# Causal attention with decay and a gated convolution: loads of the first head pair first, the activation table loaded ahead, and every order, engine, bank and buffer planned anew

## The chip, the cores and the metric

The kernel runs on one core of one Trainium2 chip. The metric is device microseconds of one execution (us), median of the runs shown. Engines: PE is the matrix engine, ACT the scalar engine, DVE the vector engine, POOL the GpSimd engine, and SP the engine that issues most of the transfers. Each engine works through its own instructions strictly in program order.

## The reference

Inputs are q, k, v of shape (8, 8, 576, 64), s of shape (8, 8, 576) and three weight arrays. Scores with a decay go through a causal softmax; the result goes through a causal five-tap convolution gate and two projections.

```python
scores = scale * np.matmul(q, k.transpose(0, 1, 3, 2))
cum = np.cumsum(np.maximum(s, 0.0), axis=-1)
bias = -(cum[:, :, :, None] - cum[:, :, None, :])
scores = np.where(causal, -1e9, scores + np.minimum(bias, 0.0))
attn = softmax(scores)                       # rows sum to 1
x = (attn @ v).transpose(0, 2, 1, 3).reshape(B, S, H * D)
gate_pre = sum(conv_w[t] * x_shifted[t] for t in range(5))
out = (sigmoid(gate_pre) * (x @ w_val)) @ w_out
```

## The kernel before

The work is cut into 32 units n = 4b + p: batch b (8 of them) and head pair p (4 each). For one unit, Q and K of two heads are loaded as float32 into a staging buffer qkf (five of them; a buffer holds two pairs; one transfer of the first pairs is 288 KB), cast to bf16 into qkb (three buffers), transposed on PE (step qq), copied out of PSUM into QKT (qe), and multiplied (scores, steps s0, s1, s2, and s4 for the last 64 queries). ACT takes exp of 128 x 1024 scores at a time (e0, e1, e2, e4) into P, of which there are three buffers. The triangle on the diagonal is cleared in one of two ways: PE adds a pair of wide matmuls of the tile fut to the scores, or POOL clears P afterwards with an affine select (mk). The decay is put into V instead of the scores: a running sum of s on DVE (relu, scan, centre), a transpose (decT) and one exp (expw) give w, and POOL multiplies V by w into Vp (vp). Then av multiplies P by Vp on PE, DVE divides by the row sum (rec, nm), PE transposes (xt), one copy goes to xT (xe), and the convolution follows as taps t1 to t4 (DVE, or POOL with a product p2 to p4 before it), tanh on ACT (th), the value projection on PE (val), the gate product on DVE (glu), and per two batches nine blocks of the output projection (out), their copies (oe) and stores (st). The last four units are split in two halves (steps u and f, with a third index on the later steps).

What sets the order is one text, ORDER: a list of steps name:engine:slots written by a planner beforehand. S, G, T, A and V are SP, POOL, PE, ACT and DVE; slots are PSUM banks or buffer numbers. The loop at the end of main_path (L731 to L746) calls each step's function in that order, with the engine that the list names, so the list fixes each engine's instruction order, which engine does a cast or a copy, which bank and which buffer it uses. Nothing is reordered later. Steps wu are matmuls of the identity that nobody reads; they keep PE busy.

The names and lines that the prediction uses: load_qk (L425) issues Q or K transfers, and ld_first those of batch 0, one head pair and one of Q and K at a time; ld_qk loads Q and K of one or two pairs of a later batch; ld_v (L448, L449 for batch 0, L452 later) loads V; ld_s (L374) the decay input, ld_cw (L396) the convolution weights. Casts, copies and evacuations all go through the helper copy (L371). vprime is L455, scores are L476 and L489 (the latter the fut matmuls), exps(step) is L527, mask L550, av L565, rec L578, norm L584, tap_product L614 (ACT) and L616 (POOL), tap L627, L632 (DVE) and L635 (POOL), tanh L652, val L664, glu L673, outp L684, stores L692.

At the end the kernel tests whether its way of computing was safe for the data: check0 and check1 (L695 to L707) test the row sums, and check0 also squares the 20 weight ratios cwr and compares them (L700, L701); count (L710) counts on PE, count_out (L719) takes the minimum, and flag (L715) reads it, so that a branch can run a general version in a rare case. That version does not run here.

Of the kernel before, what the change touches and what calls it, by code (L numbers as in the profile page):

```python
# [213 lines left out]
glu.0.0:V val.2.1:T:3 ld_v.2.4:S t1.5:V:1 e0.9:A xt.6:T:5 ld_v.2.3:S glu.3.0:V p3.5:G:1 s1.9:T:0+1 glu.2.1:V xe.6:A
ld.3.0:S:3 s1.8:T:6+7 e1.9:A t1.6:V:3 qq.2.2:T:2+3 out.0.3:T:4 t3.5:G qe.2.2:A t4.6:V out.0.2:T:0 th.4:A:4 t3.6:V
p4.5:G:0 oe.0.3:A:0 ld_v.3.3:S s0.8:T:1+2:2 oe.0.2:A:1 t2.6:V ld.3.1:S:4 qq.2.3:T:3+4 p2.5:G:1 e0.8:A xt.7:T:0 qe.2.3:V
out.0.0:T:5 e1.8:A xe.7:V t2.5:G s2.8:T:1+2 t1.7:V:2 out.0.1:T:3 e2.8:A t3.7:V vp.2.0:G val.4.1:T:4 th.6:A:1 oe.0.1:V:2
s4.2.3:T:1+2 s2.9:T:6+7 oe.0.0:A:4 t2.7:V t4.5:G val.6.1:T:3 e4.2.3:A st.0.0:S val.7.1:T:5 glu.6.1:V e2.9:A ld_v.3.2:S
val.4.0:T:1 t4.7:V vp.2.2:G st.0.3:S av0.8:T:2+3 glu.4.1:V ld_v.3.0:S th.7:A:0 val.6.0:T:0 glu.4.0:V av.8:T vp.2.1:G
th.5:A:2 glu.6.0:V s0.11:T:6+7:0 glu.7.1:V s0.10:T:0+1:2 rec.8:V e0.11:A val.5.1:T:4 nm.8:V c.3.0:G:0 val.7.0:T:5  # L220
e0.10:A xt.8:T:2 glu.7.0:V s2.10:T:6+7 c.3.1:G glu.5.1:V val.5.0:T:3 e2.10:A xe.8:V s1.10:T:0+1 glu.5.0:V ld_v.3.4:S
mk.10:G s1.11:T:4+5 t1.8:V:0 out.0.7:T:3 e1.11:A ld_v.3.1:S vp.2.3:G t4.8:V av0.9:T:6+7 e1.10:A ld.5.0:S:0 av.9:T t3.8:V
qq.3.0:T:4+5 mk.11:G oe.0.7:A:5 av0.10:T:0+1 rec.9:V qe.3.0:A nm.9:V st.0.7:S av.10:T c.3.2:G:1 ld.4.1:S:1 s0.12:T:3+4:1
# [576 lines left out]
```

## Time and profile before

| | before |
|---|---|
| median of 3 runs | 184.66 us (184.64 to 185.24) |
| the profiled execution | 185.04 us |
| its span, first to last instruction | 183.0 us |
| granted TensorE clock, mean | 0.978 |
| HBM read, written | 30.57 MB, 9.44 MB |

The profiled execution's time is 2.04 us more than its span: what lies before its first and behind its last instruction. It is 0.38 us above the median of the three runs. A page of the profile has busy times by engine, forty slices of the span with the busy share of each engine, the chain of work that ended last, and groups of instructions. In the views a row "x3" stands for three instructions merged; the bracket at a row's end says how long the engine had been idle and what released it.

### The profile page before, as it was taken

Reading aid. Unit: us, or ns where it says so; the run is one execution under the profiler, and the core shown is the slowest. Engines: PE = TensorE matmul, PEld = TensorE weight load, DVE = VectorE, ACT = ScalarE, POOL = GpSimd, SP = SyncE. Lnnn points to the kernel's source line nnn. Section 1 sums busy time; section 2 is a strip of 40 time slices with the busy share of each in tenths; the row PEclk is TensorE's granted clock in tenths of the full one; section 3 lists DMA queues with packets and bytes.
Section 4 is the critical chain, followed back from the end, with each engine's and each line's share of the span. In section 5 each row is a group of like instructions: output and inputs, shape, how many; then the busy total and the mean of one; then the engine's idle time right before and its main releaser. Section 6 shows DMA issues by size and latency. Waiting matters only on the chain.

```text
span 183.0 us, 6744 instructions
## 1 busy us (share of the span) xinstructions
PE 166.4 (91%) x2773; PEld 108.8 (59%) x2790; DVE 161.3 (88%) x311; ACT 159.0 (87%) x229; POOL 158.9 (87%) x150
## 2 busy tenths in 40 slices
PE   6499889899999999999989999999899999999950
PEld 2136765667557765665856675775567746757520
DVE  4295699999999999999999999989999999999940
ACT  0098999898999899999999999899999899998830
POOL 5289689999999989999699999889999998999800
PEclk9879999999999999999999999999999999999995
DMA  5999999999999999975899958994960014006461
GB/s 140 332 288 317 296 189 283 399 362 185 295 345 253 298 334 318 333 205 127 244 306 271 326 153 273 224 249 116 222 216 4 4 57 176 3 4 236 170 238 56
DMA packets 52812, 40.48 MB, mean 221 GB/s; under 512 B 38885, under 2 KB 38885, under 8 KB 52778
## 3 DMA queue, kind: packets, MB, share of 16 engines
q1 hardware_dynamic: 52490, 39.42, 75.4%
q10 hardware_dynamic: 288, 0.59, 1.2%
q8 instruction: 23, 0.38, 0.9%
q14 instruction: 11, 0.09, 0.2%
HBM read 30.57 MB, written 9.44 MB: 219 GB/s over the span
## 4 chain that ended last, share of the span: by engine, by line
PE 73%; ACT 11%; DVE 4%; issue 3%; DMA 3%; SPq 2%; POOL 1%; ACTq 0%; DVEq 0%; POOLq 0%
PE bank L664 18%; PE bank L684 16%; PE bank L565 13%; PE bank L476 13%; ACT P L527 7%; PE bank L597 5%; PE bank L460 5%; DMA qkf<-in_q_dram 3%; PE bank L489 2%; POOL qkb L371 1%; DVE xn L584 1%; ACT QKT L371 1%; DVE gp L632 1%; ACT th L652 1%; SPq L425 1%
## 5 line engine op out<-in xcount | busy, mean ns | idle before, releaser
L527 ACT ACTIVATE P<-bank 128x1024 bf16<-128x1024 f32 x84 | 82.9, 1037 | 1.9 <-PE bank L476 1.6
L632 DVE SCALAR_TENSOR_TENSOR gp<-bank,cwr,gp 128x572 f32<-128x572 bf16 (+6 forms) x74 | 55.0, 753 | 1.0
L635 POOL TENSOR_TENSOR gp<-gp,pr 128x573 f32<-128x573 f32 (+6 forms) x34 | 41.1, 1212 | 4.3 <-DVE recs L578 2.3
L455 POOL TENSOR_TENSOR Vp<-vst,w 128x650 bf16<-128x650 f32 x32 | 40.7, 1287 | 1.2 <-DMA vst<-in_v_dram 1.0
L476 PE MATMUL bank<-QKT 64*128 64x128 bf16 (+5 forms) x592 | 39.1, 241 | 1.7 <-ACT P L527 1.3
L664 PE MATMUL bank<-xT,wv 128*128 128x288 bf16 (+2 forms) x256 | 38.9, 287 | 0.4 <-ACT P L527 0.2
L371 POOL CAST qkb<-qkf 128x1152 bf16<-128x1152 f32 (+2 forms) x29 | 31.8, 1120 | 6.0 <-DMA qkf<-in_q_dram 5.2
L684 PE MATMUL bank<-wo,glu 128*128 128x512 bf16 x127 | 34.4, 380 | 1.8 <-issue 0.6
L565 PE MATMUL bank<-Vp,P 128*128 128x65 bf16 x960 | 34.7, 194 | 1.4 <-POOL Vp L455 1.0
L565 PEld LDWEIGHTS <-P 128*128 128x128 bf16 x960 | 32.0, 97 | 6.5 <-ACT P L527 2.5
L476 PEld LDWEIGHTS <-QKT 64*128 64x128 bf16 x592 | 19.5, 95 | 16.8 <-issue 11.5
L664 PEld LDWEIGHTS <-wv 128*128 128x128 bf16 x256 | 22.6, 97 | 10.7 <-issue 3.7
L616 POOL TENSOR_TENSOR pr<-xT,cwr 128x573 f32<-128x573 bf16 (+6 forms) x27 | 27.1, 1011 | 1.3 <-DVE xT L371 0.7
L584 DVE TENSOR_TENSOR xn<-bank,recs 128x640 bf16<-128x640 f32 (+2 forms) x36 | 26.8, 747 | 0.9
L673 DVE SCALAR_TENSOR_TENSOR glu<-th,bank 128x288 bf16<-128x288 f32 (+2 forms) x64 | 26.4, 446 | 1.1 <-PE bank L664 0.7
L627 DVE SCALAR_TENSOR_TENSOR gp<-xT,cwr,bank 128x576 f32<-128x576 bf16 (+2 forms) x36 | 26.6, 742 | 0.8
L652 ACT ACTIVATE th<-gp,cwr 128x576 f32<-128x576 f32 x28 | 21.7, 793 | 0.6 <-DVE gp L632 0.6
L684 PEld LDWEIGHTS <-glu 128*128 128x128 bf16 x144 | 12.2, 97 | 13.3 <-issue 2.0
L371 ACT COPY ot<-bank 128x512 f32<-128x512 f32 x27 | 15.8, 598 | 2.0 <-PE bank L684 1.8
L460 PE MATMUL bank<-ident,qkb 64*128 64x64 bf16 x576 | 13.8, 192 | 2.9 <-DVE qkb L371 2.5
L460 PEld LDWEIGHTS <-qkb 64*128 64x128 bf16 x576 | 10.8, 95 | 9.2 <-issue 3.4
L550 POOL TENSOR_SCALAR_AFFINE_SELECT P<-P 128x1024 bf16<-128x1024 bf16 (+1 forms) x14 | 15.0, 1078 | 1.1 <-ACT P L527 1.1
(58 smaller groups left out, 150.5 us busy)
## 6 DMA issues: line engine op xcount, KB each, us to landing
out_dram<-ot SPq DMA_DIRECT2D x36, 256.0 KB, 3.5
vst<-in_v_dram SPq DMA_DIRECT2D x28, 256.0 KB, 6.0
qkf<-in_q_dram SPq DMA_DIRECT2D x12, 576.0 KB, 7.5
qkf<-in_k_dram SPq DMA_DIRECT2D x12, 576.0 KB, 8.2
qkf<-in_q_dram SPq DMA_DIRECT2D x8, 288.0 KB, 5.2
vst<-in_v_dram SPq DMA_DIRECT2D x15, 128.0 KB, 5.4
qkf<-in_k_dram SPq DMA_DIRECT2D x6, 288.0 KB, 5.3
qkf<-in_moe_w_val_dram SPq DMA_DIRECT2D x1, 1024.0 KB, 7.7
```

What stands on the lines that cost most here:

```text
L371: (act.copy if e is act else e.tensor_copy)(dst, src)
L455: e.tensor_tensor(Vps[b % 2][:, :, HP[p]], vslot(b)[:, :, HP[p]], w[:, :, b * 8 + 2 * p:b * 8 + 2 * p + 2].unsqueeze(3).to_broadcast([128, ...
L460: return pe.transpose(out, src[64 * r:64 * r + 64, :], ident[64 * r:64 * r + 64, 64 * r:64 * r + 64])
L476: pe.matmul(ps[:, hh, c0:c0 + nq], QKTs[b % 2][r, p, k0:k0 + 128, 1], QKTs[b % 2][r, p, q0:q0 + nq, 0], **kw)
L527: act.activation(out=Pt(n)[:, :, step * 512:(step + 1) * 512], in_=pair((f"s{step}", n)), func=AF.Exp, scale=0.125)
L565: pe.matmul(ps[:, o:o + 65], lhsT, Vps[b % 2][:, kb, 2 * p + w, :], start=(kb == 0), stop=(kb == qb))
L584: vec.tensor_tensor(xns[b % 2][:, g, p * 128:(p + 1) * 128].rearrange("t g (w d) -> t w g d", w=2), ps[:, :, :, 0:64], recs[:, n, :, g].un ...
L616: pool.tensor_tensor(pr, xTs[b % 2][:, c, 4 + lo - m:4 + hi - m], r.to_broadcast([128, hi - lo]), ALU.mult)
L632: vec.scalar_tensor_tensor(gp[:, lo:hi], xps(n, *h)[:, lo - m:hi - m], r, gp[:, lo:hi], ALU.mult, ALU.add)
L635: pool.tensor_tensor(gp[:, lo:hi], gp[:, lo:hi], prs[at[f"p{m}", n, *h][0]][:, lo:hi], ALU.add)
L664: pe.matmul(ps, wv[:, dc, c * 128:(c + 1) * 128], xTs[b % 2][:, dc, 4 + lo:4 + hi], start=(dc == 0), stop=(dc == 3))
L684: pe.matmul(bank_of(u, i), glu2[:, c, i * 128:i * 128 + 128], wo[:, c, :], start=(c == 0), stop=(c == 3))
```

## The change

A new list ORDER, and two new steps in it. The list has the same attention and gate steps as before for all 32 units; other are their order on each engine, the engine for some of them, banks and buffers, and which units are masked on POOL (17 units, 14 before). The transfer of the convolution weights is moved from the first to the eleventh place of SP's queue, and Q of the first pair to the first. A step warm makes ACT copy 128 values, ahead of its other instructions. The squaring and comparing of the weight ratios moves out of check0 into a step of its own (cwk), which stands right behind the step that computes the ratios.

```diff
 ORDER = """
-ld_cw:S ldk.0.0:A ld_s:S ldk.0.1:A wu.0:T:0 wu.9:T:1 ldq.0.0:S wu.1:T:0 ldk.0.2:S wu.11:T:1 ldq.0.2:S wu.4:T:0 wu.38:T:1
+ldq.0.0:S ldk.0.0:A ld_s:S ldk.0.1:A warm:A wu.4:T:0 wu.24:T:1 ldq.0.1:S wu.9:T:0 ldq.0.2:S wu.13:T:1 ldk.0.2:S
...
@@
     vec.memset(onec, 1.0)
+    warm = one.tile([128, 1], FP32, name="warm")
@@
+    def first_act(e):
+        copy(e, warm, onec)
@@
-    def check0(e):
+    def check_ratios(e):
         rf = cwr.rearrange("p c k -> p (c k)")
         e.tensor_tensor(okt, rf, rf, ALU.mult)
         e.tensor_scalar(ok[:, 4:24], okt, 1e12, None, ALU.is_le)
+
+    def check0(e):
         extremes(e, 0, recs[:, 0:NE].rearrange("p a b c -> p (a b c)"))
@@
-    does = dict(ld_s=ld_s, relu=relu, ...
+    does = dict(warm=first_act, ld_s=ld_s, relu=relu, ...
-                chk0=check0, chk=check1, cnt=count, cntc=count_out, flag=flag)
+                cwk=check_ratios, chk0=check0, chk=check1, cnt=count, cntc=count_out, flag=flag)
```

The first place is the start of SP's queue, in which the first transfers are issued. Here qkf_133 is the buffer of pairs 0 and 1 of batch 0, qkf_134 that of pairs 2 and 3, gp_118 takes s, ot_128 the convolution weights, and vst_91 V. Before:

```order
L396 DMA ot_128<-in_moe_conv_w_dram 5x512
L374 DMA gp_118<-in_s_dram 64x576
L425 DMA qkf_133<-in_q_dram 64x2x576
L425 DMA qkf_134<-in_k_dram 64x2x576
L425 DMA qkf_134<-in_q_dram 64x2x576
L425 DMA qkf_133<-in_q_dram 64x2x576
L448 DMA vst_91<-in_v_dram 128x4x64 x2
```

And of the changed program:

```order
L429 DMA qkf_133<-in_q_dram 64x2x576
L378 DMA gp_118<-in_s_dram 64x576
L429 DMA qkf_133<-in_q_dram 64x2x576
L429 DMA qkf_134<-in_q_dram 64x2x576
L429 DMA qkf_134<-in_k_dram 64x2x576
L429 DMA qkf_134<-in_q_dram 64x2x576
L452 DMA vst_91<-in_v_dram 128x4x64 x2
L453 DMA vst_91<-in_v_dram 64x2x64
L429 DMA qkf_134<-in_k_dram 64x2x576
L400 DMA ot_128<-in_moe_conv_w_dram 5x512
```

Q of pair 0 is now the first transfer, Q of pair 1 the third instead of the sixth, and the weights come behind all of Q and K of batch 0. (K of pairs 0 and 1 is issued by ACT in both.)

The second place is POOL's program behind its set-up: casts into qkb, products Vp, masks of P. qkf_135 and qkf_136 hold pairs 2, 3 and pairs 0, 1 of batch 1. Before:

```order
L371 CAST qkb_101<-qkf_133 128x2x4x64 x2
L371 CAST qkb_102<-qkf_134 128x2x5x64
L371 CAST qkb_101<-qkf_133 128x2x5x64
L550 AFFINE_SELECT P_113<-P_113 128x2x512
L371 CAST qkb_102<-qkf_134 128x2x5x64
L455 TENSOR_TENSOR Vp_106<-vst_91,w 128x5x130 x2
L371 CAST qkb_103<-qkf_135 128x2x9x64
L455 TENSOR_TENSOR Vp_106<-vst_91,w 128x5x130
L371 CAST qkb_101<-qkf_136 128x2x9x64 x2
L455 TENSOR_TENSOR Vp_106<-vst_91,w 128x5x130
```

And of the changed program:

```order
L372 CAST qkb_101<-qkf_133 128x2x4x64
L372 CAST qkb_101<-qkf_133 128x2x5x64
L372 CAST qkb_102<-qkf_134 128x2x5x64
L459 TENSOR_TENSOR Vp_106<-vst_91,w 128x5x130
L372 CAST qkb_103<-qkf_135 128x2x9x64
L554 AFFINE_SELECT P_114<-P_114 128x2x512
L459 TENSOR_TENSOR Vp_106<-vst_91,w 128x5x130 x2
L620 TENSOR_TENSOR pr_131<-xT_110,cwr 128x574
L639 TENSOR_TENSOR gp_116<-gp_116,pr_131 128x574
L372 CAST qkb_101<-qkf_136 128x2x9x64
L372 CAST qkb_103<-qkf_135 128x2x9x64
L459 TENSOR_TENSOR Vp_106<-vst_91,w 128x5x130
```

Two parts of casts of batch 0 have left POOL, the cast of the first pair of batch 1 to be loaded (qkb_103) has come from ACT and stands directly behind the first Vp, and the mask is that of unit 1 instead of unit 0. Behind these rows come a mask (unit 6), the last cast of batch 1, a mask (unit 4), one tap, and then the first Vp of batch 1; before, it was two products and two taps.

The third place is ACT's program at its start, where qkf_133 is again the staging buffer and QKT_104 the transposed Q and K of batch 0. Before:

```order
L425 DMA qkf_133<-in_k_dram 64x2x576 x2
L527 ACT_TABLE_LOAD
L527 ACTIVATE P_113<-bank 128x2x512 x3
L503 ACTIVATE P_97<-bank 128x2x64
L392 ACTIVATE w<-bank 128x320
```

And of the changed program:

```order
L429 DMA qkf_133<-in_k_dram 64x2x576 x2
L372 ACT_TABLE_LOAD
L372 CAST warm<-onec 128x1
L372 COPY QKT_104<-bank 128x576
L531 ACTIVATE P_113<-bank 128x2x512 x2
L396 ACTIVATE w<-bank 128x320
L507 ACTIVATE P_97<-bank 128x2x64
```

The table load stands behind nothing but the two transfers, the copy of the first QKT has come from DVE to ACT, and the third exp of unit 0 stands behind the exp of w and the first of the small ones.

More of the change, by code (lines that the diff above doesn't have):

```diff
@@ L214 @@
[L214 to L223, printed above, removed]
@@ L289 @@
-oe.3.4:A:0 t4.31.1:G glu.28.1:V glu.29.1:V st.3.4:S outa.3.8:T:4 t2.31.1:V chk:V st.3.0:S th.31.1:A:3 val.31.1:T:3
-oe.3.5:A:1 glu.31.1:V out.3.8:T outa.3.7:T:0 oe.3.8:V:2 st.3.5:S cnt:T:1 out.3.7:T cntc:V st.3.8:S oe.3.7:A:4 st.3.7:S
-flag:S
+ldq.0.0:S ldk.0.0:A ld_s:S ldk.0.1:A warm:A wu.4:T:0 wu.24:T:1 ldq.0.1:S wu.9:T:0 ldq.0.2:S wu.13:T:1 ldk.0.2:S
+wu.12:T:0 wu.36:T:1 ldq.0.3:S wu.27:T:0 ld_v.0.0:S wu.33:T:1 wu.16:T:0 wu.20:T:1 wu.35:T:0 ldk.0.3:S c.0.0.0:V c.0.0.1:G
+ld_cw:S relu:V qq.0.0:T:0+1 ld.1.1.0:S:2 scan:V wu.5:T:2 qe.0.0:A wu.32:T:3 c.0.1.0:G s0.0:T:0+1:0 ld_v.0.1:S c.0.1.1:V
@@ new lines @@
+qe.2.3:A out.0.2:T:0 t3.6:V e1.8:A mk.8:G st.0.1:S xe.7:V s2.9:T:2+3 ld.5.0:S:4 oe.0.2:V:2 s2.8:T:4+5 e2.9:A t3.5:G
+val.4.1:T:6 t1.7:V:1 val.7.0:T:0 ld.3.1:S:0 e2.8:A glu.4.1:V val.4.0:T:7 vp.2.0:G t3.7:V s4.2.3:T:2+3 th.6:A:0
+ld_v.3.3:S s0.10:T:5+6:2 t4.7:V out.0.0:T:4 e4.2.3:A ld_v.3.2:S t4.5:G e0.10:A t2.7:V av0.8:T:2+3 av.8:T glu.4.0:V
+oe.0.0:A:4 vp.2.2:G val.6.0:T:1 rec.8:V th.5:A:3 nm.8:V val.5.1:T:4 th.7:A:1 s0.11:T:5+6:0 vp.2.1:G glu.5.1:V
+s2.10:T:2+3 glu.6.0:V xt.8:T:7 e2.10:A glu.7.0:V val.6.1:T:4 xe.8:V mk.10:G val.7.1:T:0 glu.6.1:V e0.11:A s1.10:T:1+2
@@ new lines @@
+t2.12:V e2.17:A t3.15:G av0.16:T:6+7 av.16:T t4.12:V ld_v.5.1:S th.14:A:2 s0.18:T:2+3:1 rec.16:V p2.15:G:0 val.14.0:T:4
+e0.18:A nm.16:V out.1.3:T:5 glu.14.0:V th.12:A:0 vp.4.2:G glu.14.1:V xt.16:T:2 oe.1.3:A:0 s1.18:T:3+4 xe.16:V
+s2.18:T:6+7 e1.18:A val.12.0:T:1 t1.16:V:0 mk.18:G val.15.0:T:5 glu.12.1:V e2.18:A t2.15:G s0.19:T:3+4:2 glu.12.0:V
+t3.16:V s4.5.3:T:0+1 e0.19:A av0.18:T:6+7 t4.16:V av.18:T c.6.2:G:0 e4.5.3:A s0.20:T:3+4:1 rec.18:V th.15:A:4
+val.13.1:T:2 nm.18:V c.6.3:G val.15.1:T:0 e0.20:A st.0.8:S glu.13.1:V xt.18:T:1 ld_v.5.4:S glu.15.0:V s2.19:T:6+7
@@ new lines @@
+xt.19:T:2 t2.17:G th.18:A:1 s1.21:T:6+7 xe.19:V val.18.0:T:0 th.16:A:2 t1.19:V:1 out.1.7:T:3 c.7.1:G oe.1.8:A:0
+glu.18.0:V e1.21:A t4.17:V val.18.1:T:4 vp.5.0:G val.16.0:T:0 glu.18.1:V oe.1.7:A:2 val.17.0:T:1 t4.19:V st.1.8:S
+th.17:A:0 qq.7.1:T:3+4 st.1.5:S vp.5.1:G glu.16.0:V qq.7.0:T:5+6 qe.7.1:A glu.17.0:V val.16.1:T:7 ld_v.6.3:S t2.19:V
+qe.7.0:A s0.22:T:0+1:0 vp.5.3:G s0.23:T:3+4:2 glu.16.1:V ld_v.6.4:S av0.21:T:5+6 e0.23:A t3.19:V av.21:T st.1.6:S
+vp.5.2:G val.17.1:T:7 rec.21:V th.19:A:3 nm.21:V av0.20:T:2+3 e0.22:A av.20:T c.7.2:G:0 glu.17.1:V ld_v.7.3:S
@@ new lines @@
+p4.30.1:G:0 glu.28.0:V val.29.1:T:1 oe.3.1:A:0 p3.31.1:G:1 t1.31.1:V:3 val.30.1:T:4 glu.30.0:V val.28.1:T:5 t4.30.1:G
+st.3.1:S val.31.1:T:3 t3.29.1:V st.3.3:S t3.31.1:G out.3.4:T:6 glu.28.1:V t3.30.1:V t2.29.1:V th.30.1:A:0 out.3.5:T:2
+t4.31.1:V oe.3.4:A:4 t4.29.1:V t2.31.1:V out.3.6:T:5 th.29.1:A:4 st.3.4:S glu.30.1:V th.31.1:A:3 st.3.0:S glu.29.1:V
+oe.3.5:A:3 glu.31.1:V outa.3.8:T:0 oe.3.6:V:5 st.3.5:S out.3.8:T chk:V st.3.6:S outa.3.7:T:1 oe.3.8:A:0 cnt:T:2
+out.3.7:T st.3.8:S cntc:V oe.3.7:A:1 st.3.7:S flag:S
@@ L719, in count_out @@
         vec.tensor_reduce(okcnt, bank[0:1, at["cnt"][0], 0:24], AX.X, ALU.min)
-    does = dict(ld_s=ld_s, relu=relu, scan=scan, centre=centre, decT=decT, expw=expw, ld_cw=ld_cw, cwT=conv_T,
+    does = dict(warm=first_act, ld_s=ld_s, relu=relu, scan=scan, centre=centre, decT=decT, expw=expw, ld_cw=ld_cw, cwT=conv_T,
                 cwc=conv_ratio, ld_wv=ld_w("ld_wv", moe_w_val), ld_wo=ld_w("ld_wo", moe_w_out),
```

159 lines of the change are left out of this document (75 added, 84 removed).

## The prediction

> **What bounds the kernel now.** I read the page's busy times first, then busy time by stretch.
>
> ```profile
> span 183.0 us, 6744 instructions
> PE 166.4 (91%) x2773; PEld 108.8 (59%) x2790; DVE 161.3 (88%) x311; ACT 159.0 (87%) x229; POOL 158.9 (87%) x150
> ```
>
> ```profile
> 10.00:20.00 10.00, 9.57 (x191) 6.30 (x190) 6.78 (x13) 9.46 (x13) 9.00 (x9) 0.94 1.07 312
> 20.00:170.00 150.00, 144.61 (x2517) 97.15 (x2531) 144.81 (x266) 144.41 (x207) 142.91 (x124) 1.00 0.79 221
> ```
>
> In the 150 us from 20 to 170 PE, DVE, ACT and POOL are busy for 144.6, 144.8, 144.4 and 142.9 us: four engines, all within 5% of full. No single engine's relief is worth its full size there, and a new order alone can win at most the 5 to 7 us that are idle. What is left is the start, so I read it next: POOL's and then ACT's rows in order of time.
>
> ```profile
> 7.26 0.93 POOL L371 CAST qkb<-qkf 128x512 bf16<-128x512 f32 x1 [3.73 <-DMA qkf<-in_q_dram]
> 9.65 3.20 POOL L371 CAST qkb<-qkf 128x512 bf16<-128x512 f32 x3 [1.46 <-DMA qkf<-in_q_dram]
> ...
> 19.54 1.28 POOL L455 TENSOR_TENSOR Vp<-vst,w 128x650 bf16<-128x650 f32 x1 [0.84 <-DMA vst<-in_v_dram]
> ...
> 22.81 1.15 POOL L371 CAST qkb<-qkf 128x1152 bf16<-128x1152 f32 x1 [0.65 <-DMA qkf<-in_k_dram]
> 24.14 1.28 POOL L455 TENSOR_TENSOR Vp<-vst,w 128x650 bf16<-128x650 f32 x1 [0.18 <-DMA vst<-in_v_dram]
> ...
> 31.09 3.75 POOL L455 TENSOR_TENSOR Vp<-vst,w 128x650 bf16<-128x650 f32 x3
> ```
>
> ```profile
> 9.52 1.28 ACT L527 ACT_TABLE_LOAD   x1 [9.52 <-DVE QKT L371]
> 10.82 2.85 ACT L527 ACTIVATE P<-bank 128x1024 bf16<-128x1024 f32 x3
> ...
> 15.08 4.79 ACT L527 ACTIVATE P<-bank 128x1024 bf16<-128x1024 f32 x5
> ```
>
> POOL is released by a transfer again and again until 24.14: the start is bound by when Q, K and V land. ACT's first exp begins at 10.82, and behind it ACT hardly pauses. So I split the run at 31.09, where POOL begins the first Vp of batch 1 and is out of the transfers' reach, into the start, the rest, and the tail.
>
> **The change part by part: the start.** Q of pair 0 is issued first instead of third on SP's queue.
>
> ```profile
> GB/s 0 0 0 0 0 0 0 0 20 31 0 81 173 173 173 369 380 415 357 357 242 242 219 207 265 311 311 276 300 254 403 403 369 357 357 380 403 369 392 411
> ```
>
> ```profile
> qkf<-in_k_dram ACTq DMA_DIRECT2D x1, 288.0 KB, 3.5
> ...
> qkf<-in_q_dram SPq DMA_DIRECT2D x1, 288.0 KB, 5.2
> ```
>
> The first row is the rate in slices of 0.2 us from 0 to 8. The first K, issued at 0.82, took 3.5 us; the first Q, issued at 1.90, took 5.2 and landed at 7.1, with the first cast behind it at 7.26. Summed, the slices give 603 thousand bytes by 4.4 us; Q and K of pair 0 are 590. Were they moved alone, both would be there at 4.4; with s (147 more) beside them, at 5.0. As nothing else is known of sharing, 7.1 (no gain) is the other end. I take 5.2, near the rate row: the first cast **2.0 us earlier**, and the first exp at about 8.5, 2.3 earlier.
>
> The table load adds little to that.
>
> ```profile
> 9.97 1.46 PE L476 MATMUL bank<-QKT 64*128 64x128 bf16 x16
> ```
>
> The first exp needs the first 8 of these 16 matmuls, which end about 10.7 (half of 1.46 behind 9.97); the load ended at 10.80. Taking it out of the way is worth 0.1, at most 0.85 (10.82 less 9.97). In the changed order one table load stands in ACT's program, in front of warm, at a time when ACT idles (9.52 us idle now), so it is hidden; the copy of the first QKT that comes to ACT is hidden by the same idle time. [...]
>
> But the same bytes must land. From 7.26 (3.5 transfers of 288 KB: K, s, K, Q) to 24.14 (all of batch 0's V, Q and K and batch 1's Q and K, 20.5) the queue delivered 17 in 16.9 us, **1.0 us each**; for the early Q and K alone it is 0.80 (three from 7.26 to 9.65, where the second row of POOL is released). In the new order POOL's second cast needs the transfers up to 4.5, the third up to 6.5, the first Vp up to 8.5 (12.2 us), and the cast of batch 1 that now stands behind it up to 11.5: landing at 15.2 by 1.0 each, and at 14.4 if Q and K take 0.80 and V what is then left of the 16.9, 1.6 each; I take 14.7. POOL waits there, with all that follows queued behind. Its rows from there to the first Vp of batch 1, by these durations:
>
> ```profile
> L455 POOL TENSOR_TENSOR Vp<-vst,w 128x650 bf16<-128x650 f32 x32 | 40.7, 1287 | 1.2 <-DMA vst<-in_v_dram 1.0 <-ACT w L392 0.2
> ...
> L371 POOL CAST qkb<-qkf 128x1152 bf16<-128x1152 f32 x24 | 27.0, 1148 | 0.8 <-DMA qkf<-in_k_dram 0.6 <-PE bank L476 0.2
> ...
> L550 POOL TENSOR_SCALAR_AFFINE_SELECT P<-P 128x1024 bf16<-128x1024 bf16 x12 | 13.3, 1113 | 1.1 <-ACT P L527 1.1
> L635 POOL TENSOR_TENSOR gp<-gp,pr 128x573 f32<-128x573 f32 x9 | 12.7, 1406 | 2.1 <-DVE recs L578 1.6
> ...
> L371 ACT COPY ot<-bank 128x512 f32<-128x512 f32 x27 | 15.8, 598 | 2.0 <-PE bank L684 1.8
> ...
> L635 POOL TENSOR_TENSOR gp<-gp,pr 128x574 f32<-128x574 f32 x7 | 9.8, 1406 | 0.9 <-DVE recs L578 0.5
> ...
> L616 POOL TENSOR_TENSOR pr<-xT,cwr 128x574 f32<-128x574 bf16 x7 | 8.0, 1146 | 0.0
> ...
> L371 DVE COPY ot<-bank 128x512 f32<-128x512 f32 x9 | 6.1, 683 | 0.5 <-PE bank L684 0.5
> ...
> L635 POOL TENSOR_TENSOR gp<-gp,pr 128x380 f32<-128x380 f32 x3 | 2.9, 987 | 0.1
> L635 POOL TENSOR_TENSOR gp<-gp,pr 128x192 f32<-128x192 f32 x5 | 2.9, 592 | 0.7 <-DVE gp L632 0.5
> ...
> L550 POOL TENSOR_SCALAR_AFFINE_SELECT P<-P 128x768 bf16<-128x768 bf16 x2 | 1.7, 866 | 0.0
> ...
> L700 DVE TENSOR_TENSOR okt<-cwr 128x20 f32<-128x20 f32 x1 | 1.0, 1040 | 0.0
> ...
> L701 DVE TENSOR_SCALAR ok<-okt 128x20 bf16<-128x20 f32 x1 | 0.8, 779 | 0.0
> ```
>
> Four casts (4.6), three masks (3.3), three Vp (3.9), a product (1.15) and two taps (2.8) are 15.75, less about 0.04 for each of 12 overlaps (three Vp took 3.75 where three times 1.287 is 3.86): 15.3. 14.7 and 15.3 are 30.0; with something for waits on masked P and on taps, 30.3, against 31.09: **-0.8**. The ends are 29.7 (-1.4), and 31.1 if the transfers give nothing (0). Of the 2.0 us at the front the pace of the transfers takes back 1.2.
>
> ld_cw is moved past all early loads, with cwT waiting for it on PE and queued behind it the scores s1.1 and the first av. It lands behind about 9.5 transfers, 12.5 to 13.2. ACT then has the exps of unit 1 to do, so it costs nothing unless later than about 15. Further wu matmuls (24 for 22) lie in PE's idle time.
>
> **The rest, from that Vp on.** I counted the steps behind it in both lists. POOL has two full masks more (2.2), one mask of a half unit less (0.87), a tap of 380 (0.99) and one of 192 (0.59) less, and one product changed from a large to a small half (about -0.4, as these two taps differ): -0.6. ACT has two exps fewer (0.95 each by the row at 10.82) and two output copies more (0.60 each): -0.7. DVE has two output copies fewer (1.4), and the two checking rows L700 and L701 (1.8) move to the start, where DVE waits for the first av: about -3, the taps roughly evened out. PE has eight wide score matmuls and two fut pairs fewer and one small score step more:
>
> ```profile
> 28.56 0.41 PE bank L476 x8
> 28.96 0.22 PE bank L489 x2
> ```
>
> 0.41 and 0.44 less, about 0.45 more: -0.4. The mean of the four is -1.2, the least -0.4. Since all four are nearly full I take the middle, **-0.8**; the ends are +0.6 (the new order idles 1 us more in 150) and -2. Where a step changes its engine it is counted on both.
>
> **The tail.**
>
> ```profile
> 174.06 0.18 DVE L695 TENSOR_REDUCE stat<-recs 128x1 f32<-128x40 f32 x1
> ...
> 174.38 0.17 DVE L707 TENSOR_SCALAR ok<-stat 128x2 bf16<-128x2 f32 x1
> ...
> 174.95 0.35 DVE L673 SCALAR_TENSOR_TENSOR glu<-th,bank 128x192 bf16<-128x192 f32 x1 [0.40 <-PE bank L664]
> ...
> 175.36 1.04 PE L684 MATMUL bank<-wo,glu 128*128 128x512 bf16 x4 [0.52 <-DVE glu L673]
> ...
> 176.33 0.17 PE L710 MATMUL bank<-ok,onec 128*1 128x24 bf16 x1
> ```
>
> The count (L710) stands on PE ahead of the last projection matmul. In the new order an output copy (0.68) and the four checks (0.49, from 174.06 to 174.55) stand on DVE behind the last glu and ahead of it: about 1.2 us, where PE has 1.04 to do meanwhile. **+0.2**, between 0 and 0.5. What follows, the last copy, store and branch, is as before.
>
> **Sum.** The profiled execution's 185.04 (2.04 beside its span of 183.0): -0.8 -0.8 +0.2 is -1.4, 183.6. It lay 0.38 above the median, 184.66, so the median comes to **183.3**.
>
> **The rivals.** (a) The whole head start is kept: transfers come at 0.80 each or less and POOL does not wait at 14.7; -2.0 at the start, -1.2 after it, 0 at the tail: 184.66 - 3.2 = 181.5. For it: ACT is the engine that runs without a pause from 10.8, and gets its first scores 2.3 us earlier. Against it: five rows of POOL released by transfers. (b) It is given back: the start is worth -0.4, the new middle idles as the ends say (+0.3), tail +0.2: 184.7. For it: in the middle four engines are full, so an order has little left to win. (c) Slower: the cast of batch 1 at POOL's head waits longer than planned, with two Vp, and so two av and the P buffers (three), queued behind it. The price is 1 us for each us beyond 14.7, as POOL's 15.3 us follow without a gap; 1.4 us eat the gain (16.1), and from 17.0 on the run is slower by over 0.5%; at 18, 186.5. For it: a V transfer kept POOL waiting for 0.84 us at 19.54, so V comes slower than 1.0, and one stands ahead of this cast. Against it: of 8 transfers between 3.5 and 11.5 only that one is V. [...]
>
> **How the numbers follow.** Forecast (182.4 to 184.3) 0.46, (a) 0.16, (b) 0.24, (c) 0.12, (d) 0.02. A measurement of this kernel can tell about 0.5% (0.9 us) from no change: faster means below 183.74, slower above 185.58. Faster: (a), (d) and 0.40 of the forecast, 0.58; slower: (c), 0.12; the rest, 0.30. The range, 181.3 to 185.2, takes in (a) and (b) at their values and leaves out (c) and the ends of (a).
>
> **What would show it right or wrong.** The first cast at 5.2 and the first exp at 8.5 (the transfers); POOL idle ahead of its second cast of Q and K of batch 1's pairs, released by a transfer at 14.7, and the first Vp of batch 1 near 30.3 (the start's term); DVE free of L700's 1.04 us around 151; busy shares from 20 to 170 still near 96% (the rest); the count at least 1.2 us behind the last glu (the tail). I am wrong if the first Vp of batch 1 is early but the end is not (then the middle gave it back), or if POOL's cast waits beyond 16.1.

## The result, and the profile after

The changed kernel took 183.41 us (median of 20 runs, 180.65 to 186.74), the kernel before 185.38 us on the same chip (20 runs, 183.74 to 186.56). The ratio is 0.9851, with a 95% interval from 0.981 to 0.9892: about 1.5% faster. The ratio leaves out runs that lie over 1.5% above the fastest of their kernel, ten of the changed kernel's 20 and one of the other's; the medians take all, and lie 1.1% apart. The forecast, 183.3 us, was met. It stood for a change of -1.4 us; the medians moved by 1.97 and the profiled executions by 1.78. Its reasons were met only in part: large errors in the sum nearly cancel.

| profiled execution | before | after |
|---|---|---|
| time | 185.04 us | 183.26 us |
| span | 183.0 us | 181.5 us |
| time outside the span | 2.04 us | 1.76 us |
| end of the last output copy | 177.44 us | 177.01 us |
| landing of the last store | 181.56 us | 179.96 us |
| mean granted clock | 0.978 | 0.975 |

Of the 1.78 us between the two profiled executions only 0.43 were won by the time the last copy ends. Another 1.17 come between that copy and the landing of the last store, and 0.28 outside the span (the span's own end gives 0.1 back).

Of the page after, the span and the busy times, and below them the two stretches by engine (busy time and instructions of PE, PEld, DVE, ACT and POOL, then the granted clock, DMA share and GB/s):

```profile
span 181.5 us, 6759 instructions
PE 166.5 (92%) x2768; PEld 110.2 (61%) x2786; DVE 163.1 (90%) x314; ACT 158.9 (88%) x229; POOL 158.7 (87%) x149
```

```profile
10.00:20.00 10.00, 8.88 (x124) 5.63 (x126) 7.16 (x13) 5.60 (x8) 6.20 (x6) 0.66 1.04 249
20.00:170.00 150.00, 144.35 (x2561) 98.62 (x2575) 144.43 (x266) 145.07 (x208) 144.32 (x125) 1.00 0.77 222
```

The middle is as full as it was (144 to 145 us of 150). From 10 to 20 us ACT is busy for 5.60 us (9.46 before), POOL for 6.20 (9.00 before), and the granted clock is 0.66 (0.94 before). Something goes wrong there. First, what went right: the rows of POOL and of ACT after, in order of time.

```profile
5.04 0.93 POOL L372 CAST qkb<-qkf 128x512 bf16<-128x512 f32 x1 [1.50 <-DMA qkf<-in_q_dram]
...
13.56 1.14 POOL L372 CAST qkb<-qkf 128x1152 bf16<-128x1152 f32 x1 [0.70 <-DMA qkf<-in_k_dram]
...
33.82 1.29 POOL L459 TENSOR_TENSOR Vp<-vst,w 128x650 bf16<-128x650 f32 x1
```

```profile
2.23 1.28 ACT L372 ACT_TABLE_LOAD   x1 [2.23 <-issue]
...
7.72 1.94 ACT L531 ACTIVATE P<-bank 128x1024 bf16<-128x1024 f32 x2 [0.71 <-PE bank L493]
11.06 0.44 ACT L396 ACTIVATE w<-bank 128x320 f32<-128x320 f32 x1 [1.40 <-PE bank L393]
```

The first cast starts at 5.04 (forecast 5.2), the first exp at 7.72 (8.5), and POOL's cast of batch 1's K at 13.56, released by a transfer, as was forecast for 14.7. But the first Vp of batch 1 stands at 33.82 instead of 30.3. ACT's row at 11.06 leads on: after only two exps ACT waits 1.40 us for L393, the transpose decT on PE. DVE's and PE's rows just before it, after:

```profile
8.69 0.87 DVE L372 CAST qkb<-qkf 128x512 bf16<-128x512 f32 x1
...
9.65 0.79 DVE L388 TENSOR_SCALAR gp<-gp,chalf 64x576 f32<-64x576 f32 x1
...
10.50 0.52 PE L393 MATMUL bank<-identf,gp 64*128 64x64 f32 x5 [1.94 <-DVE gp L388]
```

DVE does a cast of pair 1 (0.87) ahead of the centring of s (L388); PE's decT waits 1.94 us for the centring, and the transposes of pair 1 (qq.0.1) stand behind decT. And a little later the granted clock falls. Stretches of 2 us, after:

```profile
8.00:10.00 2.00, 0.56 (x5) 0.12 (x4) 1.96 (x4) 1.66 (x2) 2.00 (x2) 1.00 1.17 329
10.00:12.00 2.00, 1.50 (x46) 1.16 (x47) 0.95 (x3) 0.44 (x1) 0.56 (x2) 1.00 1.08 329
12.00:14.00 2.00, 1.40 (x18) 0.76 (x17) 1.58 (x3) 1.39 (x3) 1.30 (x2) 0.51 1.25 300
14.00:16.00 2.00, 1.99 (x25) 1.38 (x20) 1.05 (x4) 1.91 (x3) 1.81 (x3) 0.50 1.19 182
16.00:18.00 2.00, 2.00 (x27) 1.27 (x24) 1.93 (x4) 0.22 (x1) 1.25 (x1) 0.50 0.77 203
18.00:20.00 2.00, 2.00 (x22) 1.06 (x23) 1.65 (x2) 1.64 (x2) 1.28 (x1) 0.78 0.89 232
```

PE idles 1.94 us of the four from 8 to 12; from 12 to past 18 the clock is 0.50, from 14 on PE has work without a pause (1.99 to 2.00 of 2 us), and ACT is starved (0.22 us busy from 16 to 18). The single runs say the same. Of the 20 runs of the changed kernel two had a mean clock of 0.995 or more and took 180.65 and 181.22 us; five of 0.989 to 0.992, 182.63 to 182.83; seven of 0.974 to 0.977, 183.02 to 184.74; six of 0.964 to 0.972, 185.04 to 186.74.

The tail after, DVE's, PE's and ACT's rows, and the last store (KB, median us from issue to landing) before and after:

```profile
174.62 0.68 DVE L372 COPY ot<-bank 128x512 f32<-128x512 f32 x1
...
175.89 0.17 PE L716 MATMUL bank<-ok,onec 128*1 128x24 bf16 x1
...
176.43 0.59 ACT L372 COPY ot<-bank 128x512 f32<-128x512 f32 x1 [0.44 <-PE bank L688]
```

```profile
out_dram<-ot SPq DMA_DIRECT2D x1, 256.0 KB, 4.1
```

```profile
out_dram<-ot SPq DMA_DIRECT2D x1, 256.0 KB, 2.9
```

The last glu ends at 174.70, and the count (L716) follows 1.19 us behind it, where it was 1.03 before: 0.16 us more, as forecast (0.2). But the last store lands 4.1 us after its issue before, and 2.9 after. Nothing in the forecast said so.

### The profile page after: what moved, and what is told of

It reads as the page before. It is cut to its first block, busy times and chain, and to the rows that moved or that the text cites. A ratio compares the mean times of both kernels' runs of the same rounds, so it can differ in the third digit from the quotient of the medians.

```text
span 181.5 us, 6759 instructions
## 1 busy us (share of the span) xinstructions
PE 166.5 (92%) x2768; PEld 110.2 (61%) x2786; DVE 163.1 (90%) x314; ACT 158.9 (88%) x229; POOL 158.7 (87%) x149
## 4 chain that ended last, share of the span: by engine, by line
PE 68%; DVE 15%; ACT 6%; issue 4%; DMA 3%; SPq 0%; DVEq 0%; ACTq 0%
PE bank L688 16%; PE bank L668 15%; PE bank L569 14%; PE bank L480 12%; PE bank L601 5%; DVE gp L636 4%; PE bank L464 3%; ACT P L531 3%; DVE xn L588 3%; DMA gp<-in_s_dram 3%; DVE gp L631 2%; DVE QKT L372 2%; PE bank L595 2%; PE bank L493 2%; ACT QKT L372 1%
## 5 line engine op out<-in xcount | busy, mean ns | idle before, releaser
L636 DVE SCALAR_TENSOR_TENSOR gp<-bank,cwr,gp 128x573 f32<-128x573 bf16 (+6 forms) x76 | 56.0, 747 | 1.1
L639 POOL TENSOR_TENSOR gp<-gp,pr 128x574 f32<-128x574 f32 (+6 forms) x32 | 39.6, 1241 | 4.3 <-DVE recs L582 2.2
L668 PE MATMUL bank<-xT,wv 128*128 128x288 bf16 (+2 forms) x256 | 37.9, 286 | 0.1
L569 PEld LDWEIGHTS <-P 128*128 128x128 bf16 x960 | 33.0, 99 | 6.8 <-issue 2.2
L569 PE MATMUL bank<-Vp,P 128*128 128x65 bf16 x960 | 36.0, 195 | 0.3 <-ACT QKT L372 0.2
L620 POOL TENSOR_TENSOR pr<-xT,cwr 128x572 f32<-128x572 bf16 (+6 forms) x26 | 25.7, 998 | 1.3 <-ACT xT L372 1.3
L554 POOL TENSOR_SCALAR_AFFINE_SELECT P<-P 128x1024 bf16<-128x1024 bf16 (+1 forms) x17 | 18.4, 1084 | 1.0 <-ACT P L531 0.6
L372 ACT COPY ot<-bank 128x512 f32<-128x512 f32 x29 | 17.3, 602 | 1.9 <-PE bank L688 1.2
L601 PE MATMUL bank<-ident,xn 128*128 128x128 bf16 x164 | 15.0, 220 | 0.9 <-DVE xn L588 0.9
L372 ACT COPY QKT<-bank 128x576 int32<-128x576 int32 x20 | 12.7, 646 | 3.0 <-PE bank L464 2.9
```

The costliest lines, as they stand in the source:

```text
L372: (act.copy if e is act else e.tensor_copy)(dst, src)
L569: pe.matmul(ps[:, o:o + 65], lhsT, Vps[b % 2][:, kb, 2 * p + w, :], start=(kb == 0), stop=(kb == qb))
L636: vec.scalar_tensor_tensor(gp[:, lo:hi], xps(n, *h)[:, lo - m:hi - m], r, gp[:, lo:hi], ALU.mult, ALU.add)
L639: pool.tensor_tensor(gp[:, lo:hi], gp[:, lo:hi], prs[at[f"p{m}", n, *h][0]][:, lo:hi], ALU.add)
L668: pe.matmul(ps, wv[:, dc, c * 128:(c + 1) * 128], xTs[b % 2][:, dc, 4 + lo:4 + hi], start=(dc == 0), stop=(dc == 3))
```

## The experiments

Three questions were open. Does the half clock eat the head start? What is each part of the change worth? And why does the last store land sooner? Kernels of one group share a chip and the runs of the kernel before: E1 to E4 185.61 us (29 runs), E5 to E8 185.04 (19), E9 to E11 185.8 (13), E12 185.29 (17). E1 to E4 ran on one chip, E5 to E11 on a second, E12 on a third, so times of different groups are compared with care, and the steps of two profiles count for more.

| | edit | median us (lowest to highest, runs) | ratio to before, 95% interval | clock in the profile |
|---|---|---|---|---|
| E1 | after, dummy products in PE's wait | 181.06 (180.51 to 181.96, 6) | 0.9797, 0.975 to 0.9843 | 0.994 |
| E2 | before, new order of loads | 185.58 (183.32 to 187.45, 12) | 0.9976, 0.9929 to 1.0023 | 0.978 |
| E3 | before, dummy products | 185.55 (184.67 to 187.77, 12) | 1.001, 0.9978 to 1.0042 | 0.989 |
| E4 | after, ratio test late | 186.86 (184.21 to 188.65, 12) | 1.0022, 0.9973 to 1.0072 | 0.975 |
| E5 | E1, ratio test late, PE kept busy there | 182.97 (182.59 to 183.31, 10) | 0.9912, 0.9876 to 0.9948 | 0.999 |
| E6 | E1 without warm | 181.55 (180.86 to 182.53, 4) | 0.9864, 0.9774 to 0.9954 | 1.000 |
| E7 | after, decT behind qq.0.1 | 182.73 (181.11 to 184.55, 4) | 0.9868, 0.9752 to 0.9985 | 0.977 |
| E8 | after, unaltered | 183.69 (180.72 to 185.17, 10) | 0.9894, 0.9812 to 0.9977 | 0.975 |
| E9 | before, ratio test early | 184.13 (183.35 to 186.45, 4) | 0.9873, 0.981 to 0.9937 | 0.984 |
| E10 | E2, dummy products | 184.9 (184.24 to 186.97, 10) | 0.9961, 0.9923 to 0.9999 | 0.989 |
| E11 | E1, two steps of the start earlier | 180.77 (180.43 to 181.65, 4) | 0.9731, 0.9673 to 0.9789 | 0.998 |
| E12 | before, one store later | 183.92 (183.3 to 185.3, 12) | 0.9918, 0.9889 to 0.9947 | 0.997 |

### E1: the clock held at the start

```diff
-c.0.2.1:V c.0.2.0:G decT:T:6 e1.0:A
+c.0.2.1:V c.0.2.0:G wu.200:T:7 wu.201:T:7 wu.202:T:7 wu.203:T:7
+wu.204:T:7 wu.205:T:7 wu.206:T:7 wu.207:T:7 decT:T:6 e1.0:A
```

> The changed kernel with eight more matmuls of the identity that nobody reads on PE, ahead of decT, where PE waited for DVE from 8.56 to 10.50 us. Theory A (the clock): that wait is why the granted clock falls to 0.5 from about 12 to 18.5 us; filled, the mean granted clock is 0.99 or more, PE's 30 av matmuls at 15.4 take about 1.0 us instead of 1.83, and the time is 1.5 to 2.5 us below the changed kernel's 183.4, ratio to before 0.975 to 0.982. Theory B (the transfers bound the start): clock or not, the time stays within 0.4 us of the changed kernel's.

181.06 us, by the medians 2.3 us faster than the changed kernel. By the ratios to the kernel before the two lie nearer (0.9797 and 0.9851, with intervals that overlap), so the steps of the two profiles have to decide. The same stretches in E1:

```profile
8.00:10.00 2.00, 2.00 (x15) 0.81 (x12) 1.96 (x4) 1.89 (x2) 2.00 (x2) 1.00 1.16 321
10.00:12.00 2.00, 2.00 (x49) 1.22 (x47) 0.77 (x3) 0.44 (x1) 0.37 (x2) 1.00 1.07 341
12.00:14.00 2.00, 1.40 (x30) 0.98 (x22) 1.64 (x3) 1.74 (x3) 1.50 (x2) 1.00 1.27 286
```

The eight products compute nothing that is used, and decT starts no earlier (10.56). What changes is the clock, 1.00 where it was 0.51. At 22 us the steps are 2.2 us earlier than in the changed kernel, from 33 us on 2.34, and so it stays, within 0.05 us, to the last copy. The loss at the start is the half clock, and the program behind carries a shift of its start to its end undiminished.

### E2, E3, E10: the same in the kernel before

E2 gives the kernel before the new order of SP's first ten loads (its diff shows these alone, without the steps between them); E3 puts dummy products into the kernel before; E10 is E2 with dummy products in PE's two waits.

```diff
-ld_cw:S ld_s:S ldq.0.0:S ldk.0.2:S ldq.0.2:S ldq.0.1:S ld_v.0.0:S ldq.0.3:S ld_v.0.1:S ldk.0.3:S
+ldq.0.0:S ld_s:S ldq.0.1:S ldq.0.2:S ldk.0.2:S ldq.0.3:S ld_v.0.0:S ldk.0.3:S ld_cw:S ld_v.0.1:S
```

> The kernel before with only the order of its first ten transfers on SP taken from the changed kernel (Q of pair 0 first, Q of pair 1 third, convolution weights ninth); everything else as before. Theory B: the load order carries the gain, 1.5 to 2.5 us, ratio 0.986 to 0.992. Theory A: the first exp comes about 2 us earlier, but the rest of the list was planned for the other order, and the gain is 0 to 1 us, ratio 0.994 to 1.0.

```diff
+wu.200:T:0 wu.201:T:1 wu.202:T:0 wu.203:T:1 wu.204:T:0 wu.205:T:1
 qq.0.0:T:0+1
```

> The kernel before with six more matmuls of the identity ahead of the first transposes, where PE waited for the first cast from 5.25 to 7.78 us. Theory A: the half clock from about 8 to 11.3 us goes, the mean clock rises from 0.978 to 0.99 or more, and the first exp comes 0.4 to 1 us earlier; the end 0.3 to 1.0 us earlier, less than in the changed kernel because the half clock lies where PE also waits for transfers. Theory B: no difference, within 0.3 us.

```diff
+wu.200:T:7 wu.201:T:7 wu.202:T:7 wu.203:T:7 wu.204:T:7 wu.205:T:7 wu.206:T:7
 qq.0.2:T:6+7
+wu.300:T:0 wu.301:T:0 wu.302:T:0 wu.303:T:0 wu.304:T:0
 qq.0.1:T:0+1
```

> E2 (the kernel before with the new order of its first loads) with dummy products in TensorE's two waits there (1.73 and 1.29 us): seven ahead of qq.0.2, five ahead of qq.0.1. Theory A (the half clock at 12 to 16 us is what ate the head start of 2.5 us in E2): 183.2 to 184 us. Theory B (the head start is lost to the old order of the casts, since the third exp waits for GpSimd's casts of pair 0, before any half clock): 185 us or more, little better than E2.

E2 is worth nothing measurable: its first exp is 2.5 us earlier than before, the fourth 0.6 us later. E3 held the clock at 1.00 in the whole start and won nothing: in the kernel before, the same half clock (0.50 to 0.68 from 8 to 12 us) costs no time. Why is argued, not shown: there the casts behind wait for transfers anyway. E10 comes close to its theory B. The dummy products do undo a part (the fourth exp is now 0.87 us earlier than before, where it was 0.62 later in E2), but this lead, too, is gone by 30 us. POOL's rows in E10 show the first link:

```profile
14.07 2.65 POOL L458 TENSOR_TENSOR Vp<-vst,w 128x650 bf16<-128x650 f32 x2 [0.16 <-ACT w L395]
19.19 1.14 POOL L374 CAST qkb<-qkf 128x1152 bf16<-128x1152 f32 x1 [2.47 <-DMA qkf<-in_k_dram]
```

POOL waits 2.47 us for batch 1's K and casts it 1.63 us later than before (17.56, without a wait), with its Vp, casts and products queued behind. That is the rival that the prediction put into the changed kernel; it stands in the old order, and not in the new one, where POOL reaches the last casts of batch 1 later. So the early loads alone are worth at most some 0.4% in the old order. What the new order would be worth with the old loads was not run.

### E4, E5: the ratio test at its old place

```diff
-cwc:V e4.0.2:A cwk:V av0.0:T:2+3
+cwc:V e4.0.2:A av0.0:T:2+3
...
-t4.24:G chk0:V
+t4.24:G cwk:V chk0:V
```

> The changed kernel with the test of the weight ratios put back in front of check0 near the end. If the early test costs what it took in the trace (1.94 us on DVE beside POOL's Vp product, ahead of the first rec), the first rec comes about 1.5 us earlier and the start gains up to 1 us, but DVE pays 1.8 us near 151 us again: in sum 0.5 us faster to 0.5 us slower than the changed kernel. If the early test is hidden, 0.5 to 1.5 us slower.

E4 is 3.4 us slower than the changed kernel, more than the expectation allowed in either case. Up to 153 us it runs 1.31 us ahead of it (its clock fell for 3.41 us at the start instead of 6.83, and rec.0 came 0.5 us sooner); at the end it is 2.39 behind. DVE's two small operations and the POOL rows beside them in E4, and below them PE's wait and two stretches of E4:

```profile
151.97 2.77 POOL L641 TENSOR_TENSOR gp<-gp,pr 128x574 f32<-128x574 f32 x2
...
153.37 1.42 DVE L706 TENSOR_TENSOR okt<-cwr 128x20 f32<-128x20 f32 x1
...
154.69 1.14 POOL L622 TENSOR_TENSOR pr<-xT,cwr 128x573 f32<-128x573 bf16 x1
...
154.81 1.06 DVE L707 TENSOR_SCALAR ok<-okt 128x20 bf16<-128x20 f32 x1
...
156.98 0.69 PE L482 MATMUL bank<-QKT 64*128 64x192 bf16 x4 [1.59 <-DVE glu L679]
```

```profile
156.00:158.00 2.00, 0.90 (x9) 0.50 (x9) 2.00 (x7) 0.53 (x2) 1.32 (x1) 0.96 0.20 75
158.00:160.00 2.00, 2.00 (x14) 1.38 (x13) 1.36 (x4) 1.41 (x3) 1.91 (x3) 0.50 0.00 0
```

The test of 20 numbers holds DVE for 2.5 us; the glu behind it is late, PE waits 1.59 us for its bank, and then the clock halves a second time. E5 tells the two apart: dummy products at the start as in E1, the test late as in E4, and seven more products in this wait (the diff shows these seven).

```diff
+wu.300:T:3 wu.301:T:3 wu.302:T:3 wu.303:T:3 wu.304:T:3 wu.305:T:3 wu.306:T:3
 u3.28:T:1+2
```

> The changed kernel with eight dummy products ahead of decT (E1), the ratio test put back ahead of chk0, and seven dummy products on bank 3 ahead of u3.28, where TensorE waited 1.59 us for the glu behind the late test in E4. In E4 the late test cost 3.7 us between 153 and 167 us (from -1.3 to +2.4 against the changed kernel): 2.4 of it by the glu of window 27, the rest while the granted clock was 0.50 to 0.69. Theory A (the test holds VectorE 2.5 us and its gap then halves the clock): with the clock held the cost is at most the 2.4, 181.1 + 2.4 = 183.5 us or a little less. Theory B (the clock after the gap plays no part): the whole 3.7, 184.8 us. Theory C (all of the cost is the clock): 181.1 to 181.5 us.

182.97 us, 1.9 us slower than E1 by the medians (of two chips) and near theory A. The clock is 1.00 there, and the last copy is 2.2 us later than in E1, counted from where both were at 153 us. So of the 3.7 us in E4's profile some 2.2 are the test itself and its wait, and 1.5 the clock.

### E6: without warm

```diff
-ldk.0.1:A warm:A wu.4:T:0
+ldk.0.1:A wu.4:T:0
```

> E1 without the early warming of ScalarE's table. Theory A (the prediction's term: the load of 1.28 us would stand in idle time of ScalarE ahead of the first exp, worth 0.1 us): 181.1 to 181.3 us. Theory B (the first exp starts 0.7 us behind the first copy, so the load of 1.28 us delays it by some 0.6 us, and a head start of the first windows is kept to the end one for one, as the constant distances of E1 and E4 show): 181.6 to 181.8 us.

181.55 us from four runs, between the theories by its median and not to be told from E1 by its interval. The profile decides, though. ACT's rows in E6:

```profile
2.22 1.28 ACT L375 ACT_TABLE_LOAD   x1 [2.22 <-issue]
6.34 0.64 ACT L375 COPY QKT<-bank 128x576 int32<-128x576 int32 x1 [2.84 <-PE bank L467]
7.70 1.94 ACT L534 ACTIVATE P<-bank 128x1024 bf16<-128x1024 f32 x2 [0.72 <-PE bank L496]
```

Without warm the load still stands at 2.2 us and the first exp at 7.70. The copy of the first QKT, which the new order gives to ACT, has the load ahead of it, and the load didn't wait for that copy's input: it ended at 3.50 us, and PE released the copy at 6.34. So the step warm is worth nothing here, and theory B, which had the load behind the copy, is wrong about this program.

### E7: the wait cut in pieces

```diff
-c.0.2.0:G decT:T:6 e1.0:A wu.8:T:7 qq.0.1:T:0+1 expw:A
-ld_v.0.2:S qq.0.2:T:4+5
+c.0.2.0:G e1.0:A wu.8:T:7 qq.0.1:T:0+1
+ld_v.0.2:S decT:T:6 expw:A qq.0.2:T:4+5
```

> The changed kernel without dummy products, but with decT and expw behind qq.0.1 in TensorE's and ScalarE's order: TensorE's wait of 1.94 us for decT is split in one of about 1.0 us for the cast of pair 0's second quarter and one of about 0.4 us for the centring. Theory A (what halves the clock is a wait of almost 2 us in one piece): the clock stays at 1.0 through 20 us, and the time is that of E1, 181.0 to 181.6 us. Theory B (the share of idle time near 10 us counts, however it is cut up): the clock still halves, 182.5 to 183.5 us, as in the changed kernel.

Theory B: the clock halves all the same. The stretches of E7:

```profile
8.00:10.00 2.00, 1.49 (x24) 0.58 (x23) 1.96 (x4) 1.70 (x2) 2.00 (x2) 1.00 1.19 323
10.00:12.00 2.00, 1.29 (x30) 0.92 (x32) 2.00 (x4) 0.67 (x3) 0.56 (x2) 1.00 1.05 340
12.00:14.00 2.00, 2.00 (x22) 1.33 (x21) 1.39 (x5) 2.00 (x5) 1.37 (x2) 0.54 1.26 282
```

PE idles 1.2 us in pieces of up to 0.6, and the clock still falls at 12 us. (The cast that the expectation names is one of pair 1.) The median, 182.73 from four runs, can't be told from the changed kernel's. To split the wait was not enough here; with eight products in it (E1) the clock stayed at 1.00.

### E8: the changed kernel again

> The changed kernel unaltered, on the same chip as its variants. If the runs of the changed kernel differ by whether and how long the clock halves near 12 us, single runs lie between 180.6 and 187 us with the lowest clocks the slowest, median near 183.4 us; E1 is faster on the same chip by 2 us or more.

183.69 us; its profile is that of the first, half clock included: from 34 us on all steps up to the last copy lie within 0.05 us of it. E1 is 2.6 us faster, but ran on another chip; on this one stands E6, E1 without the step warm, 2.1 us faster. E1's six runs lie within 1.5 us and E5's ten within 0.7, where these ten spread over 4.5: with PE's waits filled, most of the spread is gone, too.

### E9: the early test alone

The changed program with the old ORDER, and the test where DVE waits 1.63 us for the first av.

```diff
-qe.0.3:V ld_v.0.3:S
+qe.0.3:V cwk:V ld_v.0.3:S
```

> The kernel before with its own order, and one part of the change alone: the ratio test split off and put behind qe.0.3, where VectorE waits 1.63 us (17.55 to 19.19). In the kernel before the test's two small operations hold VectorE for 1.04 and 0.78 us near 151 us; put late in the changed kernel's order they cost 1.9 us (E5 against E1). Theory A (VectorE is on the path at 151, and a delay there is kept to the end): 1.5 to 1.9 us faster than before, about 183.5 us. Theory B (the windows behind it take up the time, so that the test is worth little in the old order): within 0.5 us of before, 184.9 to 185.6 us.

The evidence is divided. The four runs have a median 1.7 us under that of before, with an interval of 0.6 to 1.9%. The two profiles differ by 0.46 us in time, and by 0.40 at the last glu: in the old order the windows behind 151 us take up most of DVE's delay. Two of the four runs had a clock of 0.999, which hardly a run of before had, so part of the median is not the test's. I hold the profile's 0.4 us for its worth in the old order, but four runs don't prove it.

### E11: a better start

E1 with the third exp of unit 0 ahead of expw, and s1.1 ahead of av0.0.

```diff
-qq.0.1:T:0+1 expw:A
+qq.0.1:T:0+1 e2.0:A expw:A
...
-cwk:V av0.0:T:2+3
+cwk:V s1.1:T:0+1 av0.0:T:2+3
```

> E1 with two moves at the start: e2.0, whose scores are ready at 8.5 us, goes ahead of expw on ScalarE, which waits there for 1.2 us, and s1.1 goes ahead of av0.0 on TensorE, so that e1.1 doesn't wait 0.5 us for it. Theory A (a head start of ScalarE's first exps is kept one for one to the end): 0.5 to 1.0 us faster than E1, 180.1 to 180.6 us. Theory B (from 19 us on VectorE sets the pace, which these moves do not touch): as E1, 180.8 to 181.4 us.

As E1, and so theory B: 180.77 against 181.06, with overlapping intervals (these two are the fastest kernels of the study, ahead of both before and after). The exp e1.1 did come 0.62 us earlier, but from 20 us on the steps are some 0.45 us later than in E1. In this run batch 1's K landed later (POOL's cast at 14.26 instead of 13.42), the mask behind it ended at 16.45, and DVE's test, which lasts as long as that mask, at 16.48 instead of 15.73, with the first rec queued behind it. So what follows the start hangs on DVE here, and the early test is not quite hidden.

### E12: one store moved

```diff
-oe.3.6:A:5 t3.30.1:V out.3.4:T:1 t3.29.1:G t3.28.1:V st.3.6:S t1.31.1:V:1
+oe.3.6:A:5 t3.30.1:V out.3.4:T:1 t3.29.1:G t3.28.1:V t1.31.1:V:1
...
-st.3.5:S cnt:T:1
+st.3.5:S st.3.6:S cnt:T:1
```

> The kernel before with one step moved: st.3.6 goes from ahead of st.3.4 to behind st.3.5, its place in the changed kernel, so that the last five stores lie closer together. In the five profiles with the old order the last store lands 3.7 to 3.9 us after its issue, and its last 8 packets of 2 KB come one by one behind an instruction fetch that began 0.6 to 0.9 us after the issue; in the eight with the new order it lands after 2.1 to 2.9 us, with the fetch later. Theory A (the order of the last stores decides what the fetch gets ahead of): landing after 2.1 to 2.9 us, 0.9 to 1.6 us faster than before, about 184.3 us. Theory B (the fetch gets ahead of the last store's packets whatever the stores before it; then this gain of the changed kernel comes from elsewhere in its order): landing after 3.7 us, no difference to before within 0.5 us.

Theory A: 183.92 us, 1.37 us faster than before by the medians. The gain lies wholly behind the last copy, which ends 0.64 us later than in the profile of before. The transfers by queue (packets, MB, share of 16 engines' time), first of before from 178.5 to 180 us, then of before from 180 to 181.5:

```profile
q1 hardware_dynamic: 102, 0.18, 33.4%
q8 instruction: 1, 0.02, 5.4%
q14 instruction: 2, 0.02, 3.1%
```

```profile
q1 hardware_dynamic: 9, 0.02, 4.6%
```

And of E12 from 178.5 to 180 us:

```profile
q1 hardware_dynamic: 258, 0.46, 85.1%
q8 instruction: 1, 0.02, 4.0%
```

Before, the stores (q1) ebb away by 179; one instruction fetch takes 1.3 us of one engine's time (5.4% of 16 engines for 1.5 us), two more follow, and then nine last packets come one by one up to 181: one engine's share of the last store, by an estimate (its 128 rows on the 16 engines that the rows count are 8 for each), and one more. In E12 the five last stores lie closer together, the stores' packets run on without a gap, the fetch begins only at 179.98, in the last slice of 25 ns before 180, and after 180 there are none of the stores' packets left. Its last store landed 2.45 us after its issue began, 4.1 before (2.1 and 3.8 from the issue's end, from which the expectation counts). That each engine's packets wait in line behind the fetch is how I read these rows (before, the fetch runs from 178.73 to 180.04, and the first of the nine packets starts at 180.02); what sets the moment of the fetch was not tried.

## Why the prediction was right

Its time was right, and the terms were these. Positions are those of the profiled executions, after less before.

**The front of the start: right.** The first cast was forecast 2.0 us earlier and came 2.2 earlier, the first exp 2.3 and came 3.1. POOL's cast of batch 1 waited for its transfer until 13.56, not 14.7; rival (c) did not occur.

**The start's term, -0.8: wrong, and here a step failed.** At the last but one of the large exps of the whole units the changed kernel is 0.90 us behind (141.56 against 140.66). Since the orders differ, this distance changes from exp to exp, from -1.8 to +3.1 from 27 us on, 0.9 in the mean and 0.74 at the last one; so the split into start and rest is good to about 1 us. The step that failed is the sum of POOL's rows from 14.7 to the first Vp of batch 1: it took POOL's work as the path and gave PE only "idle time", in which the dummy matmuls lie. POOL's 15.3 us of rows took 20.3 (13.56 to 33.82), and still 18.1 in E1 (13.42 to 31.49), which ends sooner. PE was the path: its wait of 1.94 us for decT, with qq.0.1 behind it, and the half clock that follows. E1 takes the half clock away and is 1.44 us ahead of before at that same exp. The time of rival (a), the whole head start kept, 181.5, is near E1's 181.06 and near two runs of the changed kernel itself (180.65 and 181.22). But that is in part luck: up to the last copy E1 is 2.8 us ahead of before, where (a) had 3.2, and 1.8 more come behind that copy, where (a) had nothing. The marker was badly chosen, too: the first Vp of batch 1 stands behind other work in the new order, and E1, which is faster, has it only at 31.49, later than the kernel before (31.09).

**The rest, -0.8: right in sign, by this split too small.** From that exp to the last glu the distance goes from +0.90 to -0.60, -1.5. The ratio test's removal from 151 us is in it. At its late place in the new order the test would cost some 2 us (E5 against E1: 1.9 by the medians, 2.2 by the steps), in the old one it costs some 0.4 (E9's profile). What else of the rest the new order won was not tried by itself. That the test is hidden at its new place is nearly right: beside POOL it held DVE up to 17.28, and E4 without it had the first rec 0.5 us sooner; with the clock held it cost nothing in E1 (E5, which has it late, is 0.30 us behind E1 just ahead of the first rec, and 0.30 at that rec).

**The table load, 0.1: right for the wrong reason.** The load is out of the way, but not by warm (E6). For the rival (d), which the chances take in with 0.02, no run shows a term: in the kernel before the first exp starts 0.02 us behind the load, and in the new one the load ends 4.2 us ahead of the first exp.

**The tail, +0.2: right** (0.16 at the count). **"What follows, the last copy, store and branch, is as before": wrong.** The last store lands 1.17 us sooner after its copy, and E12 shows that the place of one store is worth as much in the kernel before (1.37 us). The 0.28 us outside the span remain unexplained; the profiled executions with the old order have 1.9 to 2.1 us there, those with the new one 1.7 to 1.8.

So the sum, -1.4, was met by -1.78 because a start that was 1.7 us worse than forecast stood beside a rest that was 0.7 better and a store that was not in the sum at all (-1.17, and -0.28 outside). That these come so near to nothing together is luck. Without the store the changed kernel would have won some 0.4 us up to the last copy. The chance for faster (0.58) was the largest and came true; the argument behind it was not good enough to be sure.

## What to carry to other kernels

When a new order moves work to an earlier time, look at what PE does while it waits for the one late input: a wait of 1.94 us at the start cost 2.3 us in half clock, and eight products that nobody reads won them back. What was left of a shift at 34 us was carried to the end one for one (E1, and E4 up to 153 us), while an earlier lead can be lost before that (E10, E11). So the first 30 us deserve the closest reading, on every engine and not only on the one that waits for transfers. And read the stretch behind the last computation as a stage of its own: the place of one store was worth 0.8% there.
